# A seven-product down-projection whose partial sums are carried on by copies in PSUM

## The chip, the cores and the metric

The kernel runs on one core of a Trainium2 chip. The metric is the time of one execution on the device, in microseconds (us); less is better. Each run is one execution; a separate execution is recorded by the hardware profiler, and all rows quoted here are of that one.

## The reference

Tokens x of shape (2, 1, 4096, 640) go through two branches that a gate mixes per token. Branch A is a spectral block: a Fourier transform over the 4096 positions, a small two-layer complex network with soft thresholding per frequency and block of channels, and the inverse transform. Branch B is a gated feed-forward network with 640 channels and 1728 hidden units.

```python
def _A_ref(x, w1, b1, w2, b2):
    Xf = rfft2(x, axes=(1, 2))
    ...
    return irfft2(Yf, s=(H, W), axes=(1, 2))

def _B_ref(x, w_gate, w_up, w_down):
    return (_gelu(x @ w_gate) * (x @ w_up)) @ w_down

g = _sigmoid((x * gate_w).sum(-1, keepdims=True))
return g * _A_ref(...) + (1 - g) * _B_ref(...)
```

All of it is fp32.

## The kernel before

Every fp32 matrix product is made of three products of rounded parts (high x high, low x high, high x low). For an operand, ScalarE writes the high part (`high`, line 285) and VectorE subtracts it from the operand for the low part (`low`, line 288).

The change lies in the last stage, the down-projection together with the last step of the inverse transform. It runs in 32 iterations i, one for each batch b and each pair of token groups (na, 32 - na); an iteration makes two output rows, u1 and u2, of 128 tokens and 640 channels each. Iteration 0 has a branch of its own. The down-projection of an iteration is a 2 x 2 block product (two token groups, two halves of the hidden units, two halves c1, c2 of the channels) done with seven products in place of eight, after Winograd. The operands are the blocks a11, a12, a21, a22 of the hidden activations and sums of them: s3 = a11 - a21, s2 = a22 - s3, s1 = a11 + s2, s4 = a12 - s2. The weights are b11, b21, b22 and the combinations t1 to t4, made earlier. The seven products are a11 b11, s2 t2, s3 t3, a12 b21, s1 t1, a22 t4 and s4 b22, each of 20 or 21 matmuls of 128 x 320 into one PSUM bank. The sums that are wanted, with g1, g2 the gate of a token:

- u1, c1: a11 b11 + a12 b21
- u2, c2: a11 b11 + s2 t2 + s3 t3 + s1 t1
- u2, c1: a11 b11 + s2 t2 + s3 t3 + a22 t4
- u1, c2: a11 b11 + s2 t2 + s1 t1 + s4 b22

In an iteration the inverse transform (`inv2`, 12 matmuls of line 307, 24 where na is 0) comes first and leaves branch A's share in the SBUF tiles uu. Then `down` does six of the products in three pairs, with the matmuls of a pair interleaved over two banks (`duo`, line 1421), and the seventh alone (`run`, line 572). The partial sums that several outputs share go to an SBUF tile e: ScalarE copies a11 b11 there (line 1433), and VectorE adds s2 t2, s3 t3, a22 t4 and s4 b22 from their banks (lines 1437, 1442, 1478, 1490). VectorE also adds each finished sum, times the gate, to uu (`scaled`, line 1426), from a bank or from e.

The operands of later products are prepared between the products by `hooks[0]` to `hooks[7]`, which the program calls in the code's order:

- `h_op` makes the high and the low part of one block, tiles called ho in the profile. The low part is two or three VectorE instructions: a piece of 128 x 640 first, which the second matmul of a product already reads, and small ones.
- `h_s4` (VectorE, line 1350) makes s4; `h_s3`, `h_s2`, `h_s1` (GpSimd, lines 1332, 1339, 1344) make the sums for the next iteration n, two instructions each.
- `h_load`, `c_load` (SyncE's DMA queue) load the next iteration's blocks and its transformed rows; `v_load` (GpSimd's DMA queue, line 1194) loads the next matrix of the inverse transform; `c_split` makes four pairs of high and low parts of the transformed rows, called s2s.
- `st` notes a store of an output row, and `flush` (hooks 0 and 5) issues the noted ones on SyncE's queue.

Each engine works its queue in the order of the code and waits only for what an instruction needs: its operands, or the last reader of a buffer that it overwrites. GpSimd's queue in an iteration is: the DMA issue of v, h_s3, h_s2, h_s1.

Of the kernel before, what the change touches and what calls it, by code (L numbers as in the profile page):

```python
# [12 lines left out]
AF = mybir.ActivationFunctionType  # L13
# [208 lines left out]
def spectral_mix_kernel(ctx: ExitStack, tc: tile.TileContext, a):  # L222
    nc = tc.nc
    out = a["out"]
# [10 lines left out]
    def bank():  # L235
        return psum.tile([P, 512], F32, name="bank", tag="bank")
# [13 lines left out]
    def small(shape, dt=F32, name="small"):  # L250
        return pool.tile(shape, dt, name=name, tag="small", bufs=18)
# [7 lines left out]
    def st(dst, src):  # L259
        late.append((dst, src))  # L260
# [34 lines left out]
    def by_two(m):  # L295
        return m.rearrange("p (k i) -> p i k", k=2)
# [273 lines left out]
    def run(dst, ops, first=True):  # L570
        for i, (l, r) in enumerate(ops):
            nc.tensor.matmul(dst, l, by_two(r), start=first and i == 0, stop=i == len(ops) - 1, skip_group_check=True)  # L572
            while inner and i == 1:
                inner.pop()()
# [104 lines left out]

    PB, E = {}, []  # L680

# [289 lines left out]
    SC, Z, ZL1, ZL2, H, Y, NY = {}, {}, {}, {}, {}, {}, {}  # L971
# [214 lines left out]
    c_seq = [(b, na) for b in range(2) for na in range(16)]  # L1186
# [166 lines left out]
    def h_op(i, name, eng=nc.vector):  # L1353
        t = big([P, 5, 2, P], F32R, name="ho")
        uh, ul = (tiny([P, 2, P], F32R, name="ho") for k in range(2))
        src, six = HR[i].pop(name) if name in ("s1", "s3", "s4", "a22") else HR[i][name]
        split(t[:, :, 0], t[:, :, 1], src, eng)
        high(uh, six)
        if name in HALF:
            low(ul[:, 0], six[:, 0], uh[:, 0], eng)  # L1360
            low(uh[64:, 1], six[:64, 1], uh[:64, 1], eng)
        else:
            low(ul, six, uh, eng)
        HO[i, name] = [(t[:, j, 0], t[:, j, 1]) for j in range(5)] + [(uh[:, j], ul[:, j]) for j in range(2)]
# [25 lines left out]
                                               op0=OP.mult, op1=OP.add)  # L1390
        return uu

    def down(i, u, hooks):
        b, na = c_seq[i]
        n1, n2 = toks(na)
        g1, g2 = gs[:, b, 1, n1:n1 + 1], gs[:, b, 1, n2:n2 + 1]
        u1, u2 = u[n1], u[n2]
        c1, c2 = slice(0, 320), slice(320, 640)
        acc = lambda: bank()[:, :320]

        def rows(a_, b_):
# [10 lines left out]
        def duo(X, x, Y, y, hook, more=False):  # L1412

            n = [0, 0]
            hx, hy = rows(*x), rows(*y)
            tot = [sum(map(len, h)) for h in (hx, hy)]
            for j, (p, q) in enumerate(zip(hx, hy)):
                if j == 4:
                    hook()
                for k, (l, r) in ((0, p[0]), (0, p[1]), (1, q[0]), (0, p[2]), (1, q[-1]), *([(1, q[1])] if len(q) == 3 else ())):  # L1420
                    nc.tensor.matmul((X, Y)[k], l, by_two(r), start=n[k] == 0 and not (more and k), stop=n[k] == tot[k] - 1,  # L1421
                                     skip_group_check=True)
                    n[k] += 1

        def scaled(dst, x, g):
            nc.vector.scalar_tensor_tensor(dst, x, g, dst, op0=OP.mult, op1=OP.add)  # L1426
        hooks[0]()
        e = small([P, 2, 320], name="e")
        A = acc()
        if i:  # L1430
            Dd = acc()
            duo(A, ("a11", "b11"), Dd, ("a22", "t4"), hooks[1])
            nc.scalar.activation(e[:, 0], A, AF.Copy)
            hooks[2]()
            B, E = acc(), acc()
            duo(B, ("s2", "t2"), E, ("s1", "t1"), hooks[3])
            nc.vector.tensor_add(e[:, 0], B, e[:, 0])
            scaled(u2[:, c2], E, g2)
            hooks[4]()
            C = acc()  # L1440
            duo(C, ("s3", "t3"), A, ("a12", "b21"), hooks[5], True)
            nc.vector.tensor_add(e[:, 1], C, e[:, 0])
            scaled(u2[:, c2], e[:, 1], g2)
            scaled(u1[:, c1], A, g1)
        else:
            run(A, blk("a11", "b11"))
            nc.scalar.activation(e[:, 0], A, AF.Copy)
            hooks[1]()
            B = acc()
            run(B, blk("s2", "t2"))  # L1450
            nc.vector.tensor_add(e[:, 0], B, e[:, 0])
            hooks[2]()
            C = acc()
            run(C, blk("s3", "t3"))
            nc.vector.tensor_add(e[:, 1], C, e[:, 0])
            for u_, c_, x, g in ((u2, c2, 1, g2), (u2, c1, 1, g2), (u1, c2, 0, g1)):
                scaled(u_[:, c_], e[:, x], g)
            hooks[3]()
            F = acc()
            run(F, blk("s4", "b22"))  # L1460
            scaled(u1[:, c2], F, g1)
            hooks[4]()
            run(A, blk("a12", "b21"), first=False)
            scaled(u1[:, c1], A, g1)
            hooks[5]()
            Dd = acc()
            run(Dd, blk("a22", "t4"))
            scaled(u2[:, c1], Dd, g2)
            hooks[6]()
            E = acc()  # L1470
            run(E, blk("s1", "t1"))
            scaled(u1[:, c2], E, g1)
            st(out[b, n1], u1)
            scaled(u2[:, c2], E, g2)
            st(out[b, n2], u2)
            hooks[7]()
            return
        nc.vector.tensor_add(e[:, 1], Dd, e[:, 1])
        scaled(u2[:, c1], e[:, 1], g2)
        st(out[b, n2], u2)  # L1480
        hooks[6]()
        if i == len(c_seq) - 1:
            st(out[b, n1, :, c1], u1[:, c1])
            scaled(u1[:, c2], e[:, 0], g1)
            run(E, blk("s4", "b22"), first=False)
            scaled(u1[:, c2], E, g1)
            st(out[b, n1, :, c2], u1[:, c2])
            return
        run(E, blk("s4", "b22"), first=False)
        nc.vector.tensor_add(e[:, 0], E, e[:, 0])  # L1490
        scaled(u1[:, c2], e[:, 0], g1)
        st(out[b, n1], u1)
        hooks[7]()


# [79 lines left out]
    for k, (b, n2) in enumerate(a_seq):  # L1575
        i, j = steps_a[k]
# [46 lines left out]
    for i, key in enumerate(keys):  # L1623
# [18 lines left out]
        for j, t in enumerate(quads):  # L1642
            def hook(k):
                for f in slots.get((i, 7 * j + k), ()):
                    f()
# [7 lines left out]
            n = len(late)  # L1653
# [21 lines left out]
    uu, ahead = {}, {}  # L1675
    todo = {}
    for ch in range(1, 2 * NCH):
        b, c = chunks[ch]
# [23 lines left out]
    for i in range(S + 2):  # L1702
        events(i, 0)
        flush()
        if i < S:
# [5 lines left out]
            more = mlp1(*steps[i], sums if i + 1 < S else lambda: None)  # L1711
# [17 lines left out]


    SEQ = dict(enumerate(("s3", "s4", "a12", "a22", "s1")))
    DUO = {0: "s1", 2: "s3", 3: "a12", 4: "s4"}
    for i in range(len(c_seq)):
        n = i + 1 if i + 1 < len(c_seq) else None
        if i:
            uu = ahead if i == 1 else inv2(i)

        def step(k):
            def f():
                if (i, k) == (0, 0):  # L1740
                    wd_load(5, 5)
                    wd_later()
                if (i, k) == (0, 2):
                    ahead.update(inv2(1))
                if k in (0, 5):
                    flush()
                if k == (1 if i else 0):
                    h_s4(i)
                op = (SEQ if i == 0 else DUO).get(k)
# [22 lines left out]
        down(i, uu, [step(k) for k in range(8)])  # L1772
    flush()


# [19 lines left out]
```

## Time and profile before

| what | value |
|---|---|
| median of 3 runs | 2466.82 us (2465.4 to 2467.61) |
| the profiled execution | 2466.74 us, of which the span of the trace is 2465.0 us |
| down-projection, start of iteration 2 to start of iteration 31 | 1812.9 to 2439.3 us of the span |
| granted TensorE clock | 1.0 throughout |

A row of the timeline reads: start, length in us, engine, line, operation, what it writes and reads (buffer numbers left out), shape, count of equal instructions merged in the row, and in brackets how long the engine had been idle and what ended that. In a row of a group the numbers behind the bar are its busy time, the mean length of one in ns, and the idle time ahead of it. PE is TensorE, PEld its weight loads, DVE VectorE, ACT ScalarE, POOL GpSimd, SP SyncE.

### The profile page before, as it was taken

The page shows a single profiled execution, that of the slowest core. Times are in us where ns is not written, and L with a number is a line of the kernel's source. Part 1 is how long each engine was busy: PE and PEld are TensorE (multiplying, and loading weights), DVE is VectorE, ACT ScalarE, POOL GpSimd, SP SyncE. Part 2 cuts the span into 40 slices and gives each one's busy share as a digit, 9 for nine tenths or more (in the row PEclk, how much of TensorE's full clock was granted, in tenths as well). Part 3 has the DMA queues.
Part 4 walks back from the last instruction along what each step waited for, and adds up shares of the span by engine and source line. Part 5 has one row for each costly group of instructions (what it writes and reads, how often), then busy time and mean ns, then how long its engine had stood idle before and what let it go on. Part 6 is the DMA issues. An engine that isn't in the chain of part 4 may idle for free.

```text
span 2465.0 us, 54653 instructions
## 1 busy us (share of the span) xinstructions
PE 2445.0 (99%) x20239; PEld 2430.0 (99%) x20239; DVE 2065.8 (84%) x4323; ACT 1486.9 (60%) x3503; POOL 390.5 (16%) x404
## 2 busy tenths in 40 slices
PE   9999999999999999999999999999999999999999
PEld 9999999999999999999999999999999999999999
DVE  7777788777777877877767888888899999999998
ACT  5555556666666666666556788888744454455443
POOL 0111100000000000000003111111043334333342
PEclk9999999999999999999999999999999999999999
DMA  6666667777778687777677446467854444544443
GB/s 208 212 229 214 242 208 232 224 263 236 250 236 261 196 257 250 237 227 248 222 234 234 148 139 174 147 173 244 308 176 145 140 150 156 167 161 153 148 145 112
DMA packets 351422, 499.50 MB, mean 203 GB/s; under 512 B 26028, under 2 KB 223276, under 8 KB 351156
## 3 DMA queue, kind: packets, MB, share of 16 engines
q1 hardware_dynamic: 333684, 445.02, 56.1%
q0 software_dynamic: 17472, 51.00, 5.7%
q8 instruction: 159, 2.61, 0.4%
q14 instruction: 107, 0.88, 0.1%
HBM read 307.10 MB, written 188.81 MB: 201 GB/s over the span
## 4 chain that ended last, share of the span: by engine, by line
PE 71%; DVE 19%; issue 5%; DMA 3%; ACT 2%; SPq 0%; DVEq 0%; ACTq 0%
PE bank L572 48%; PE bank L307 11%; DVE ho L288 7%; PE bank L1421 6%; DVE s2s L288 3%; PE bank L993 3%; DVE uu L1426 2%; PE bank L704 2%; DVE uu L1389 1%; PE bank L827 1%; DVE hs L1350 1%; DMA s<-scr 1%; PE bank L1079 0%; PE bank L1080 0%; DMA xraw<-in_xT_dram 0%
## 5 line engine op out<-in xcount | busy, mean ns | idle before, releaser
L572 PE MATMUL bank<-xo,w 128*128 128x256 f32 x11196 | 1298.3, 275 | 3.1 <-ACT u L598 1.5
L572 PEld LDWEIGHTS bank<-xo,w 128*128 128x128 f32 x11196 | 1276.1, 192 | 5.9 <-ACT u L598 2.1
L1421 PE MATMUL bank<-wx,ho 128*128 128x320 f32 x3844 | 532.4, 300 | 5.6 <-DVE ho L288 5.5
L1421 PEld LDWEIGHTS bank<-wx,ho 128*128 128x128 f32 x3844 | 524.4, 189 | 10.2 <-DVE ho L288 10.0
L285 ACT ACTIVATE ho<-hraw 128x640 fp32r<-128x640 f32 x320 | 168.3, 574 | 118.5 <-PE bank L1421 83.7
L288 DVE TENSOR_TENSOR ho<-hraw,ho 128x640 fp32r<-128x640 f32 (+3 forms) x384 | 226.8, 632 | 6.4 <-ACT ho L285 3.4
L598 ACT ACTIVATE u<-bank 128x256 f32<-128x256 f32 x328 | 125.4, 382 | 161.2 <-PE bank L572 154.7
L288 DVE TENSOR_TENSOR xs<-xr,xs 64x640 fp32r<-64x640 f32 x128 | 105.0, 820 | 75.9 <-ACT xs L285 73.4
L650 DVE TENSOR_TENSOR u<-bank,u 128x256 f32<-128x256 f32 x204 | 85.9, 421 | 79.8 <-ACT u L598 78.7
L288 DVE TENSOR_TENSOR xo<-xraw,xo 128x512 fp32r<-128x512 f32 x194 | 133.3, 688 | 17.0 <-ACT xo L285 15.7
L307 PE MATMUL bank<-wm,h 128*128 128x320 f32 (+1 forms) x792 | 129.7, 300 | 0.5 <-DVE h L1057 0.4
L829 DVE TENSOR_TENSOR as<-bank,as 64x320 f32<-64x320 f32 x256 | 113.9, 484 | 18.3 <-ACT as L828 16.4
L285 ACT ACTIVATE xo<-xraw 128x512 fp32r<-128x512 f32 x194 | 121.7, 627 | 8.4 <-DMA xraw<-in_xT_dram 7.3
L598 ACT ACTIVATE p<-bank 128x256 f32<-128x256 f32 x144 | 55.3, 384 | 104.6 <-DVE h L661 57.7
L288 DVE TENSOR_TENSOR s2s<-s,s2s 128x320 fp32r<-128x320 f32 x128 | 115.7, 963 | 2.4 <-ACT s2s L285 1.5
L307 PEld LDWEIGHTS bank<-wm,h 128*128 128x128 f32 (+1 forms) x792 | 111.8, 186 | 2.1 <-DVE h L1057 0.6
L572 PE MATMUL bank<-wx,ho 128*128 128x320 f32 x764 | 110.4, 300 | 0.9 <-DVE ho L288 0.9
L285 ACT ACTIVATE xs<-xr 64x640 fp32r<-64x640 f32 x128 | 93.9, 734 | 28.2 <-DMA xr<-in_x_dram 26.4
L828 ACT ACTIVATE as<-bank 64x320 f32<-64x320 f32 x256 | 96.9, 427 | 20.3 <-PE bank L827 15.4
L572 PEld LDWEIGHTS bank<-wx,ho 128*128 128x128 f32 x764 | 105.7, 189 | 2.1 <-DVE ho L288 2.1
L780 POOL MEMSET h<- 64x512 f32 x16 | 8.3, 522 | 614.2 <-DVE h L665 178.2
L599 ACT ACTIVATE h<-bank 128x256 f32<-128x256 f32 x204 | 77.8, 381 | 29.4 <-PE bank L572 27.8
(196 smaller groups left out, 3892.8 us busy)
## 6 DMA issues: line engine op xcount, KB each, us to landing
xo<-xD SPq DMA_DIRECT2D x124, 512.0 KB
xraw<-in_xT_dram SPq DMA_DIRECT2D x215, 256.0 KB
hD<-h SPq DMA_DIRECT2D x184, 256.0 KB
hraw<-hD SPq DMA_DIRECT2D x128, 320.0 KB
xD<-xo POOLq DMA_DIRECT2D x64, 512.0 KB, 3.6
sc<-scr SPq DMA_DIRECT2D x65, 320.0 KB
xr<-in_x_dram SPq DMA_DIRECT2D x64, 320.0 KB
scr<-as SPq DMA_DIRECT2D x64, 320.0 KB
```

The source lines that it names most:

```text
L285: nc.scalar.activation(dst, src, AF.Copy, scale=scale)
L288: eng.tensor_sub(dst, src, hi.bitcast(F32))
L307: nc.tensor.matmul(dst, l, by_two(r), start=i == 0, stop=i == len(ops) - 1)
L572: nc.tensor.matmul(dst, l, by_two(r), start=first and i == 0, stop=i == len(ops) - 1, skip_group_check=True)
L598: copy = lambda d, s_: nc.scalar.activation(d, s_, AF.Copy)
L599: gelu = lambda d, s_: nc.scalar.activation(d, s_, AF.Gelu_apprx_tanh)
L650: nc.vector.tensor_add(u4, C, u4)
L704: nc.tensor.matmul(acc, l, by_two(r), start=first and i == 0, stop=i == 2, skip_group_check=True)
L828: nc.scalar.activation(stg[hi, cs], pa[lo, :320], AF.Copy)
L829: nc.vector.tensor_add(stg[hi, cs], pa[hi, :320], stg[hi, cs])
L993: nc.tensor.matmul(pz.rearrange("p (r e k f) -> p k r e f", r=2, e=2, k=4)[:, kp], SC[b, c, kp][:, o:o + P], ft.rearrange("p (r e f) -> p ...
L1421: nc.tensor.matmul((X, Y)[k], l, by_two(r), start=n[k] == 0 and not (more and k), stop=n[k] == tot[k] - 1, skip_group_check=True)
```

## The change

For iterations 1 to 31 the seven products are done one by one, in the order a11 b11, s2 t2, a12 b21, s3 t3, s1 t1, a22 t4, s4 b22, and the tile e is gone. Three PSUM banks, taken in iteration 0 and written there by matmuls, stay reserved as B, C and E2. ScalarE copies the bank of a11 b11 (A) to B; s2 t2 is added onto B by TensorE; ScalarE copies B to C; s3 t3 is added onto C; ScalarE copies C to E2; a22 t4 is added onto E2, s4 b22 onto B, a12 b21 onto A. VectorE then only adds finished banks, times the gate, to uu: six instructions in place of nine. s1 t1 has a bank of its own, E, which is added to two outputs. The inverse transform of the iteration is called behind a11 b11 and the first copy (`between`). The operands are prepared in the order of their new use, and h_s4 and s4's parts follow accordingly.

```diff
+            B, C, E2 = seeds
+            A = acc()
+            run(A, blk("a11", "b11"))
+            nc.scalar.activation(B, A, AF.Copy)
+            u = between()
...
+            hooks[1]()
+            run(B, blk("s2", "t2"), first=False)
+            nc.scalar.activation(C, B, AF.Copy)
+            hooks[2]()
+            run(A, blk("a12", "b21"), first=False)
+            scaled(u1[:, c1], A, g1)
+            hooks[3]()
+            run(C, blk("s3", "t3"), first=False)
+            nc.scalar.activation(E2, C, AF.Copy)
...
+            scaled(u2[:, c2], C, g2)
+            hooks[4]()
+            E = acc()
+            run(E, blk("s1", "t1"))
+            scaled(u2[:, c2], E, g2)
+            scaled(u1[:, c2], E, g1)
+            hooks[5]()
+            run(E2, blk("a22", "t4"), first=False)
+            scaled(u2[:, c1], E2, g2)
+            st(out[b, n2], u2)
+            hooks[6]()
+            run(B, blk("s4", "b22"), first=False)
+            scaled(u1[:, c2], B, g1)
...
-            duo(A, ("a11", "b11"), Dd, ("a22", "t4"), hooks[1])
-            nc.scalar.activation(e[:, 0], A, AF.Copy)
...
-            duo(B, ("s2", "t2"), E, ("s1", "t1"), hooks[3])
-            nc.vector.tensor_add(e[:, 0], B, e[:, 0])
...
-            duo(C, ("s3", "t3"), A, ("a12", "b21"), hooks[5], True)
-            nc.vector.tensor_add(e[:, 1], C, e[:, 0])
...
-    DUO = {0: "s1", 2: "s3", 3: "a12", 4: "s4"}
+    LATER = {0: "a12", 1: "s3", 2: "s1", 3: "a22", 4: "s4"}
...
-                if k == (1 if i else 0):
+                if k == (3 if i else 0):
                     h_s4(i)
...
                     if k == 6:
-                        h_op(n, "a22")
+                        h_op(n, "s2")
                         h_s1(n, nc.gpsimd)
-                    if k == 7:
-                        h_op(n, "s2")
```

What stands in the queues then, first on VectorE, ahead of the low part of s4 (the last operand of an iteration). In the names, ho<-hraw and ho<-hs are low parts of blocks, s2s<-s those of the transformed rows, hs<-hraw is h_s4, and uu<-bank a scaled sum. Before, from the low part of s3 on:

```order
L288 TENSOR_TENSOR ho<-hraw,ho 128x5x128
L288 TENSOR_TENSOR ho<-hraw,ho 128x256
L288 TENSOR_TENSOR ho<-hraw,ho 128x5x128
L288 TENSOR_TENSOR ho<-hraw,ho 128x128
L288 TENSOR_TENSOR ho<-hraw,ho 64x128
L288 TENSOR_TENSOR s2s<-s_30887,s2s 128x320
L288 TENSOR_TENSOR s2s<-s_30889,s2s 128x320
L288 TENSOR_TENSOR s2s<-s_30887,s2s 128x320
L288 TENSOR_TENSOR s2s<-s_30889,s2s 128x320
L1437 TENSOR_TENSOR e<-bank,e 128x320
L1426 SCALAR_TENSOR_TENSOR uu<-bank,gs,uu 128x320
L288 TENSOR_TENSOR ho<-hs,ho 128x5x128
```

The first two are s3, the next three a12; the addition into e waits for the product s2 t2. On VectorE after, from the scaled sum of A on:

```order
L1416 SCALAR_TENSOR_TENSOR uu<-bank,gs,uu 128x320
L1350 TENSOR_TENSOR hs<-hraw,hs 128x640
L1350 TENSOR_TENSOR hs<-hraw,hs 128x256
L288 TENSOR_TENSOR ho<-hraw,ho 128x5x128
L288 TENSOR_TENSOR ho<-hraw,ho 128x128
L288 TENSOR_TENSOR ho<-hraw,ho 64x128
L288 TENSOR_TENSOR s2s<-s_30506,s2s 128x320
L288 TENSOR_TENSOR s2s<-s_30508,s2s 128x320
L288 TENSOR_TENSOR s2s<-s_30506,s2s 128x320
L288 TENSOR_TENSOR s2s<-s_30508,s2s 128x320
L1416 SCALAR_TENSOR_TENSOR uu<-bank,gs,uu 128x320
L288 TENSOR_TENSOR ho<-hs,ho 128x5x128
```

The first row waits for the end of a12 b21; h_s4 now stands behind it, then the low part of a22, the four s2s and the scaled sum of C (which waits for s3 t3), and then s4's low part. On GpSimd, one iteration before, with the engines or queues waited for:

```order
L1194 DMA v<-in_v_dram 128x256 [waits DVE_49]
L1332 TENSOR_TENSOR hraw<-hraw 128x640 [waits DMAHW7_49,DMAHW1_49]
L1332 TENSOR_TENSOR hraw<-hraw 128x256 [waits DMAHW2_49,DMAHW0_49]
L1339 TENSOR_TENSOR hs<-hraw 128x640 [waits DMAHW3_49,Pool_49]
L1339 TENSOR_TENSOR hs<-hraw 128x256 [waits DMAHW4_49,PE_49,Pool_49]
L1344 TENSOR_TENSOR hraw<-hs,hraw 128x640 [waits DVE_49,Pool_49]
L1344 TENSOR_TENSOR hraw<-hs,hraw 128x256 [waits DMASW2_49,DVE_49,Pool_49]
```

On GpSimd after, the same seven:

```order
L1194 DMA v<-in_v_dram 128x256 [waits PE_49]
L1332 TENSOR_TENSOR hraw<-hraw 128x640 [waits DMAHW7_49,DMAHW3_49,DMAHW1_49]
L1332 TENSOR_TENSOR hraw<-hraw 128x256 [waits DMAHW2_49,DMAHW0_49,DMASW5_49]
L1339 TENSOR_TENSOR hs<-hraw 128x640 [waits DMAHW3_49,DVE_49,Pool_49]
L1339 TENSOR_TENSOR hs<-hraw 128x256 [waits DVE_49,DMAHW4_49,Activation_49,Pool_49]
L1344 TENSOR_TENSOR hraw<-hs,hraw 128x640 [waits DVE_49,Pool_49]
L1344 TENSOR_TENSOR hraw<-hs,hraw 128x256 [waits DVE_49,Pool_49]
```

Their order stays. The buffer that v is loaded into was last read by VectorE's low part of s3 before; after, it is a small tile of a12 that TensorE reads last, in the seventeenth of the 20 matmuls of a12 b21.

More of the change, by code (lines that the diff above doesn't have):

```diff
@@ L1428, in down @@
+        u1, u2 = u[n1], u[n2]
         e = small([P, 2, 320], name="e")
         A = acc()
-        if i:
-            Dd = acc()
-            duo(A, ("a11", "b11"), Dd, ("a22", "t4"), hooks[1])
-            nc.scalar.activation(e[:, 0], A, AF.Copy)
-            hooks[2]()
-            B, E = acc(), acc()
-            duo(B, ("s2", "t2"), E, ("s1", "t1"), hooks[3])
-            nc.vector.tensor_add(e[:, 0], B, e[:, 0])
-            scaled(u2[:, c2], E, g2)
-            hooks[4]()
-            C = acc()
-            duo(C, ("s3", "t3"), A, ("a12", "b21"), hooks[5], True)
-            nc.vector.tensor_add(e[:, 1], C, e[:, 0])
[L1443 to L1477, printed above, removed]
@@ L1491, in down @@
-        scaled(u1[:, c2], e[:, 0], g1)
-        st(out[b, n1], u1)
+        run(A, blk("a11", "b11"))
+        nc.scalar.activation(e[:, 0], A, AF.Copy)
+        hooks[1]()
+        B = seeds[0]
+        run(B, blk("s2", "t2"))
+        nc.vector.tensor_add(e[:, 0], B, e[:, 0])
+        hooks[2]()
+        C = seeds[1]
+        run(C, blk("s3", "t3"))
+        nc.vector.tensor_add(e[:, 1], C, e[:, 0])
+        for u_, c_, x, g in ((u2, c2, 1, g2), (u2, c1, 1, g2), (u1, c2, 0, g1)):
+            scaled(u_[:, c_], e[:, x], g)
@@ new lines, in down @@
+        hooks[3]()
+        F = acc()
+        run(F, blk("s4", "b22"))
+        scaled(u1[:, c2], F, g1)
+        hooks[4]()
+        run(A, blk("a12", "b21"), first=False)
+        scaled(u1[:, c1], A, g1)
+        hooks[5]()
+        Dd = seeds[2]
+        run(Dd, blk("a22", "t4"))
+        scaled(u2[:, c1], Dd, g2)
+        hooks[6]()
+        E = acc()
+        run(E, blk("s1", "t1"))
+        scaled(u1[:, c2], E, g1)
+        st(out[b, n1], u1)
+        scaled(u2[:, c2], E, g2)
+        st(out[b, n2], u2)
```

45 lines of the change are left out of this document (16 added, 29 removed).

## The prediction

> **What bounds the kernel now.** I read the page first, then the last stage by itself.
>
> ```profile
> span 2465.0 us, 54653 instructions
> PE 2445.0 (99%) x20239; PEld 2430.0 (99%) x20239; DVE 2065.8 (84%) x4323; ACT 1486.9 (60%) x3503; POOL 390.5 (16%) x404
> ```
>
> The share of TensorE says little about who sets the pace, so the next view is the table of stretches, cut from the start of iteration 2 of the down-projection to the start of iteration 31 (columns: length, then busy time of PE, PEld, DVE, ACT and POOL, the granted clock, DMA).
>
> ```profile
> 1812.90:2439.30 626.40, 621.80 (x4539) 616.84 (x4538) 614.01 (x1041) 308.78 (x667) 238.39 (x203) 1.00 0.46 154
> ```
>
> VectorE is busy 614.0 of 626.4 us (98%), ScalarE 49%, GpSimd 38%. Two engines are full here, TensorE and VectorE. TensorE's timeline tells which waits for which.
>
> ```profile
> 1793.91 16.43 PE L1421 MATMUL bank<-wx,ho 128*128 128x320 f32 x119 [0.82 <-DVE ho L288]
> ...
> 1812.89 1.79 PE L307 MATMUL bank<-s2s,v 128*128 128x320 f32 x12
> ...
> 1857.34 0.84 PE L1421 MATMUL bank<-wx,ho 128*128 128x320 f32 x5
> 1858.68 16.43 PE L1421 MATMUL bank<-wx,ho 128*128 128x320 f32 x119 [0.50 <-DVE ho L288]
> ...
> 1899.86 1.79 PE L307 MATMUL bank<-s2s,v 128*128 128x320 f32 x12
> 1901.49 17.04 PE L1421 MATMUL bank<-wx,ho 128*128 128x320 f32 x124
> 1918.37 2.88 PE L572 MATMUL bank<-wx,ho 128*128 128x320 f32 x20
> 1921.08 1.79 PE L307 MATMUL bank<-s2s,v 128*128 128x320 f32 x12
> ...
> 2115.30 3.42 PE L307 MATMUL bank<-s2s,v 128*128 128x320 f32 x24
> ...
> 2439.28 1.79 PE L307 MATMUL bank<-s2s,v 128*128 128x320 f32 x12
> ...
> 2441.94 16.43 PE L1421 MATMUL bank<-wx,ho 128*128 128x320 f32 x119 [0.19 <-DVE ho L288]
> ```
>
> An iteration without a wait lasts 1921.08 - 1899.86 = 21.22 us for 156 matmuls, 0.136 each. The 29 iterations from 1812.89 to 2439.28 take 626.39 us; 29 x 21.22 and 1.63 for the 12 extra matmuls of the row with x24 make 617.0. The rest, 9.4 us, is waiting, always at the sixth matmul of the first pair of products, for the low part of a22 from VectorE. With 0.8 in iteration 1 and 0.2 in iteration 31 that is 10.4 us: all that this stage can give back if its matmuls stay the same. Without it the execution would take 2466.7 - 10.4 = 2456.3 us.
>
> **The change, part by part.** The sum is made against the profiled execution, 2466.74 us, 0.1 below the median of the runs.
>
> Matmuls: the same seven products and the same 12 for the inverse transform, 156 per iteration. That products come one after another costs nothing: the 20 matmuls of s4 b22 already run alone on one bank, 1918.37 to 1921.08, 0.136 each, as in the pairs.
>
> VectorE's combining work, priced by shape in that stretch (busy us, mean ns):
>
> ```profile
> L288 DVE TENSOR_TENSOR ho<-hraw,ho 128x640 fp32r<-128x640 f32 x145 | 118.9, 820 | 4.4 <-ACT ho L285 3.4
> L1426 DVE SCALAR_TENSOR_TENSOR uu<-e,gs,uu 128x320 f32<-128x320 f32 x88 | 71.7, 814 | 3.1
> L1426 DVE SCALAR_TENSOR_TENSOR uu<-bank,gs,uu 128x320 f32<-128x320 f32 x58 | 31.2, 538 | 0.0
> L1490 DVE TENSOR_TENSOR e<-bank,e 128x320 f32<-128x320 f32 x29 | 14.3, 492 | 0.9
> L1478 DVE TENSOR_TENSOR e<-bank,e 128x320 f32<-128x320 f32 x29 | 13.8, 475 | 0.0
> L1433 ACT ACTIVATE e<-bank 128x320 f32<-128x320 f32 x29 | 12.7, 437 | 123.6 <-PE bank L1421 123.6
> ```
>
> Before: four additions of 0.48, three scaled sums from e of 0.81, two from a bank of 0.54, 5.4 us. After: six from a bank, 3.2 us. VectorE gets 2.2 us per iteration back. ScalarE gets two copies more of some 0.44, 0.9 us on an engine that is half idle. Copying onto a bank has no row; bounds are 0.44 and, taken as slow as the slowest other bank read of that size here, 0.54. I take 0.44; either is covered, since between a copy's source and the product that adds onto it lie 12, 20 and 21 matmuls (1.6 to 2.9 us). Only iteration 1, whose inverse transform was done early, has nothing between: 0.7 us once (copy and two hand-overs).
>
> So far this reads as a gain. What speaks against it is when VectorE's work falls, and what GpSimd does then. Two stretches of the timeline:
>
> ```profile
> 2127.73 1.70 DVE L288 TENSOR_TENSOR s2s<-s,s2s 128x320 fp32r<-128x320 f32 x4
> ...
> 2129.93 2.24 POOL L1332 TENSOR_TENSOR hraw<-hraw 128x640 f32<-128x640 f32 x2
> 2130.17 0.54 DVE L1426 SCALAR_TENSOR_TENSOR uu<-bank,gs,uu 128x320 f32<-128x320 f32 x1
> 2130.62 4.93 DVE L288 TENSOR_TENSOR ho<-hs,ho 128x640 fp32r<-128x640 f32 x3
> 2132.12 2.23 POOL L1339 TENSOR_TENSOR hs<-hraw 128x640 f32<-128x640 f32 x2
> ...
> 2168.93 2.41 DVE L288 TENSOR_TENSOR ho<-hraw,ho 128x640 fp32r<-128x640 f32 x5
> ...
> 2172.23 2.79 POOL L1332 TENSOR_TENSOR hraw<-hraw 128x640 f32<-128x640 f32 x2 [1.27 <-DMA hraw<-hD]
> ...
> 2175.21 3.05 DVE L288 TENSOR_TENSOR ho<-hs,ho 128x640 fp32r<-128x640 f32 x3
> ...
> 2182.57 1.34 DVE L288 TENSOR_TENSOR ho<-hraw,ho 128x640 fp32r<-128x640 f32 x3
> ...
> 2188.91 1.15 DVE L1350 TENSOR_TENSOR hs<-hraw,hs 128x640 f32<-128x640 f32 x2
> ...
> 2189.98 3.80 DVE L288 TENSOR_TENSOR ho<-hraw,ho 128x640 fp32r<-128x640 f32 x5
> 2191.43 0.57 POOL L1194 DMA_DIRECT2D v<-in_v_dram  x1 [9.64 <-DVE ho L288]
> 2192.09 2.28 POOL L1332 TENSOR_TENSOR hraw<-hraw 128x640 f32<-128x640 f32 x2
> 2193.81 4.01 DVE L288 TENSOR_TENSOR s2s<-s,s2s 128x320 fp32r<-128x320 f32 x4
> ...
> 2198.60 1.33 DVE L288 TENSOR_TENSOR ho<-hs,ho 128x640 fp32r<-128x640 f32 x3
> ```
>
> The same four s2s subtractions take 1.70 us alone and 4.01 beside GpSimd; the same three pieces of s4's low part 1.33 and 4.93. The scaled sum at 2130.17, which reads a bank, takes its usual 0.54 under a running GpSimd instruction. So a VectorE instruction with two SBUF tensors stands still while GpSimd computes, and one with a PSUM operand does not. From 2189.98 to the end of s4's low part at 2199.93 VectorE takes 9.95 us. Free, the same row of work is 2.41 + 1.70 + 0.48 + 0.54 + 1.33, less 0.08 for each of four overlaps, 6.14. Price of GpSimd's four subtractions (h_s3, h_s2): 3.8 us. From 2168.93, where GpSimd came late (DMA), to 2178.26 it is 9.33, a price of 3.2.
>
> The Trainium skill (SBUF — State Buffer, section "SBUF: two separate sides") calls the port pair of the two engines an exclusive lock, held for a whole instruction, which blocks the loser fully. That rule would charge the four at full length, 2.24 + 2.23 = 4.5 us, and the sum below would end at 2509 by it; the rows charge 3.8.
>
> Now the new order on VectorE. The scaled sum of A waits for the end of a12 b21; behind it, in order, stand h_s4 (1.15), a22's low part (1.34), the four s2s (1.70), the scaled sum of C (0.54), and the first piece of s4's low part (0.82), which TensorE needs at the second matmul of the seventh product. Free: 0.54 + 1.15 + 1.34 + 1.70 + 0.54 + 0.82 less five overlaps of 0.08 is 5.7, and 0.1 to wake, 5.8 us. TensorE, from the end of a12 b21, has s3 t3, s1 t1, a22 t4 and one matmul to do, 63 x 0.136 = 8.6 us. That would fit. But GpSimd's release moves too: its queue has v's DMA issue first, which waited for the low part of s3 and now waits for the seventeenth matmul of a12 b21, 0.4 us ahead of that product's end. With 0.3 to wake (as now: s3's two pieces end 1.15 after 2189.98, v follows at 2191.43) and 0.57 for the issue, h_s3 starts 0.6 us after the end of a12 b21, unless its operands land later.
>
> When they land hangs on SyncE, which issues the loads behind the two stores of the iteration before. A row of it (both stores), and two of ScalarE, whose high parts come ahead of VectorE's low parts:
>
> ```profile
> 2161.63 2.70 SPq L264 DMA_DIRECT2D out_dram<-uu  x2
> ...
> 2188.97 1.97 ACT L285 ACTIVATE ho<-hraw 128x640 fp32r<-128x640 f32 x4
> 2190.84 1.54 ACT L285 ACTIVATE s2s<-s 128x320 fp32r<-128x320 f32 x4
> ```
>
> Now the second store is out at 2164.3 and the latest h_s3 starts 7.9 us behind it, at 2172.23, held by its operands. In the new order the second store needs the sum of B. From the first piece of s4's low part VectorE has 0.5 of that part, two sums of E (1.1), a11's pair (1.15), the sum of E2 (0.5), s2's pair (1.15) beside h_s1 (some 1.6) and the sum of B (0.5) ahead of it: 6.5, less some 0.5 of overlaps, while TensorE needs 2.6 for the rest of s4 b22: the store goes 3.4 us into the next iteration. With 7.9 that is 11.3; a12 b21 ends 74 x 0.136 = 10.1 into it. So h_s3 starts 0.6 to 1.2 us after that product's end, and all four subtractions fall into it: 5.8 + 3.8 and some 0.05 to restart TensorE make 9.65, and TensorE stands 9.65 - 8.57 = 1.08 us before s4 b22, in each iteration.
>
> Bounds of that wait: 0.5 with the late GpSimd's 3.2, 1.75 with 4.5, nothing if GpSimd came so late that s4's part is ready first. I take 3.8, since GpSimd starts as early in the row as at 2192.09. The rest of the period has room: a11's low part, the tightest, is out half a microsecond ahead of its product, and VectorE is idle about 1 us before it waits for A again. ScalarE's 1.97 and 1.54 (high parts and s2s) fill 3.5 of the 5.6 us between two of its copies, so it is not late.
>
> Sum: 2456.3 (all present waits gone) + 30 iterations with a follower x 1.08 = 32.4 + 0.7 = 2489 us, 0.9% slower.
>
> **Rivals.** *VectorE's relief decides.* If no more than 2.7 us of GpSimd's work falls ahead of s4's low part, TensorE never waits and the time is 2456 to 2458, 0.4% faster. For it: 2.2 us of VectorE's 21 per iteration go, and every present wait is for VectorE. Against it: the place of v's issue, which puts h_s3 right at the head of the row. It decides above 2.7 us. The Trainium skill (Perfetto Trace Analysis, Optimizing Scalar/DVE Operations) has the same rule: where VectorE is saturated, move work to ScalarE. By it this rival would be the forecast.
>
> *The lock is longer.* A piece blocked by all four, as at 2130.62, stops h_s4 and with it a22's low part too; a wait of 1.75 per iteration, 2456.3 + 52.5 + 0.7 = 2509.
>
> *The copies are late.* If ScalarE reached each of three copies only when TensorE wants it, 0.44 + 0.3 three times in 31 iterations, 69 us, 2525. Against it: 3.5 us of its own work between copies 5.6 us apart. Here belongs the skill's advice to rotate products through banks so that a copy hides (Perfetto Trace Analysis, Optimizing Tensor Performance); the chain keeps other products between.
>
> **How the numbers follow.** A wait of 0.5 to 1.75 before s4 b22: 0.75, of which 0.1 near the long end (0.5 gives 2456.3 + 15 + 0.7 = 2472); late copies 0.03; relief 0.15; between relief and the forecast, a wait near 0.35, which just repays the gain: 0.07. A measurement of this kernel tells 0.2% (4.9 us) from nothing. The range leaves out the copies, the far end of the lock and a little of the relief: 2458 to 2509; the likeliest case alone is 2472 to 2509.
>
> **What would show it.** Right: PE waits `<-DVE ho` of about 1 us ahead of one product in each iteration, the wait at the sixth matmul gone, VectorE at 93 to 96%, GpSimd's h_s3 beginning within 2 us of the scaled sum of A, s2s and h_s4 slow beside it. Wrong: h_s3 seen 4 us or more behind that sum, or the s2s back at 0.43 each.

## The result: 2499.6 us, 1.3% slower

The changed kernel takes 2499.57 us (median of 4 runs, 2498.80 to 2500.68), the kernel before, beside it, 2467.05: ratio 1.0133, 95% interval [1.0116, 1.0151]. The forecast was 2489, the range 2458 to 2509.

Page of the changed kernel's profiled execution (2500.68 us), span and engines:

```profile
span 2498.9 us, 54472 instructions
PE 2452.7 (98%) x20239; PEld 2431.1 (97%) x20239; DVE 2056.6 (82%) x4230; ACT 1504.0 (60%) x3565; POOL 395.0 (16%) x404
```

VectorE has 9.2 us less to do in all and the kernel is slower. The table of stretches, cut as before from one inverse transform to another, that of iteration 2 to that of iteration 31 (length, then PE, PEld, DVE, ACT, POOL):

```profile
1812.34:2476.57 664.23, 630.56 (x4539) 619.04 (x4538) 610.17 (x955) 327.12 (x725) 243.09 (x203) 1.00 0.43 145
```

664.2 us where there were 626.4; VectorE is at 92% where it was at 98%. With 617.0 us of matmuls in the 29 iterations, TensorE now stands 47.2 us, 1.63 per iteration; before it was 9.4. Its timeline shows where:

```profile
2157.36 1.79 PE L307 MATMUL bank<-s2s,v 128*128 128x320 f32 x12
2158.99 11.57 PE L572 MATMUL bank<-wx,ho 128*128 128x320 f32 x84
2170.77 2.98 PE L572 MATMUL bank<-wx,ho 128*128 128x320 f32 x20 [0.21 <-DVE ho L288]
2174.76 5.70 PE L572 MATMUL bank<-wx,ho 128*128 128x320 f32 x40 [1.00 <-DVE ho L288]
2180.30 1.79 PE L307 MATMUL bank<-s2s,v 128*128 128x320 f32 x12
2181.93 14.62 PE L572 MATMUL bank<-wx,ho 128*128 128x320 f32 x104
2197.54 5.70 PE L572 MATMUL bank<-wx,ho 128*128 128x320 f32 x40 [0.99 <-DVE ho L288]
2203.07 1.79 PE L307 MATMUL bank<-s2s,v 128*128 128x320 f32 x12
...
2476.57 1.79 PE L307 MATMUL bank<-s2s,v 128*128 128x320 f32 x12
```

The stop ahead of the row with x40 is the second matmul of s4 b22 (19 of that product, then 21 of the next a11 b11); the one ahead of the row with x20 is a22 t4. The brackets give less than the loss: 20 matmuls take 2.72 us, and from 2170.77 to 2174.76 there are 3.99, a loss of 1.27 where the row shows 1.00. The list of waits has the same two views for the whole stretch, and PEld, the weight loads, comes nearer to 47.2:

```profile
PEld bank L572 <- DVE ho L288: 45.2, 48, 2.2
PE bank L572 <- DVE ho L288: 33.6, 46, 1.9
```

VectorE and GpSimd in the first of these iterations, from the scaled sum of A on:

```profile
2164.63 0.57 POOL L1194 DMA_DIRECT2D v<-in_v_dram  x1 [9.24 <-PE bank L572]
2164.76 0.55 DVE L1416 SCALAR_TENSOR_TENSOR uu<-bank,gs,uu 128x320 f32<-128x320 f32 x1 [0.47 <-PE bank L572]
2165.22 2.23 POOL L1332 TENSOR_TENSOR hraw<-hraw 128x640 f32<-128x640 f32 x2
2165.23 4.75 DVE L1350 TENSOR_TENSOR hs<-hraw,hs 128x640 f32<-128x640 f32 x2
2167.41 1.55 POOL L1339 TENSOR_TENSOR hs<-hraw 128x640 f32<-128x640 f32 x1
2169.91 1.33 DVE L288 TENSOR_TENSOR ho<-hraw,ho 128x640 fp32r<-128x640 f32 x3
2171.27 2.24 DVE L288 TENSOR_TENSOR s2s<-s,s2s 128x320 fp32r<-128x320 f32 x4
2171.47 0.88 POOL L1339 TENSOR_TENSOR hs<-hraw 128x256 f32<-128x256 f32 x1 [2.51 <-ACT ho L285]
2173.43 0.54 DVE L1416 SCALAR_TENSOR_TENSOR uu<-bank,gs,uu 128x320 f32<-128x320 f32 x1
2173.89 1.33 DVE L288 TENSOR_TENSOR ho<-hs,ho 128x640 fp32r<-128x640 f32 x3
```

GpSimd issues v and starts h_s3 0.46 us after the scaled sum of A. VectorE's h_s4, 1.15 us when free, takes 4.75: its first piece waits until three GpSimd instructions are through; the four s2s take 2.24 instead of 1.70, beside the fourth. The first piece of s4's low part is out at 2174.70 (2173.89 and 0.81), 9.94 us after 2164.76, and TensorE goes on at 2174.76.

Not every iteration is like this one. Of the 28 between 1835 and 2470 us, 16 have the long hold (h_s4's first piece 4.4 us, row 9.92 to 9.94). In ten, h_s3 starts 0.5 to 3.0 us behind the scaled sum, when that piece has already started, and the piece takes its free 0.82; nine of these have a row of 9.34 to 9.58. The mean row is 9.79.

### The profile page after: what moved, and what is told of

The parts are those of the page before. It is cut to its first block, busy times and chain, and to the rows that moved or that the text cites. A ratio compares the mean times of both kernels' runs of the same rounds, so it can differ in the third digit from the quotient of the medians.

```text
span 2498.9 us, 54472 instructions
## 1 busy us (share of the span) xinstructions
PE 2452.7 (98%) x20239; PEld 2431.1 (97%) x20239; DVE 2056.6 (82%) x4230; ACT 1504.0 (60%) x3565; POOL 395.0 (16%) x404
## 4 chain that ended last, share of the span: by engine, by line
PE 80%; DVE 14%; DMA 2%; ACT 2%; issue 2%; SPq 0%; DVEq 0%; POOL 0%; ACTq 0%
PE bank L572 60%; PE bank L307 12%; DVE hs L1350 4%; DVE ho L288 3%; DVE s2s L288 3%; PE bank L993 3%; PE bank L704 2%; PE bank L827 1%; DMA hraw<-hD 1%; DVE uu L1416 1%; PE bank L1079 1%; PE bank L1080 1%; DMA xraw<-in_xT_dram 0%; DMA scr<-as 0%; DVE w L288 0%
## 5 line engine op out<-in xcount | busy, mean ns | idle before, releaser
L288 DVE TENSOR_TENSOR ho<-hraw,ho 128x640 fp32r<-128x640 f32 (+3 forms) x384 | 216.9, 599 | 37.0 <-ACT ho L285 35.0
L285 ACT ACTIVATE ho<-hraw 128x640 fp32r<-128x640 f32 x320 | 163.1, 572 | 9.6 <-DMA hraw<-hD 4.0
L1422 ACT ACTIVATE bank<-bank 128x320 f32<-128x320 f32 x31 | 13.1, 422 | 201.8 <-DVE uu L1416 193.4
L288 DVE TENSOR_TENSOR ho<-hs,ho 128x640 fp32r<-128x640 f32 (+3 forms) x160 | 125.7, 816 | 4.0 <-ACT ho L285 2.9
L1416 DVE SCALAR_TENSOR_TENSOR uu<-bank,gs,uu 128x320 f32<-128x320 f32 x191 | 101.4, 545 | 20.1 <-PE bank L572 18.6
L1350 DVE TENSOR_TENSOR hs<-hraw,hs 128x640 f32<-128x640 f32 x64 | 111.4, 1780 | 0.0
L1344 POOL TENSOR_TENSOR hraw<-hs,hraw 128x640 f32<-128x640 f32 (+1 forms) x62 | 88.8, 1450 | 139.7 <-DVE ho L288 139.7
```

What stands on the lines that cost most here:

```text
L285: nc.scalar.activation(dst, src, AF.Copy, scale=scale)
L288: eng.tensor_sub(dst, src, hi.bitcast(F32))
L1344: eng.tensor_add(d["a11"][k], d["s2"][k], d["a11"][k])
L1350: nc.vector.tensor_sub(d["s2"][k], d["a12"][k], d["s2"][k])
```

## The experiments

Theory 1: the row on VectorE from the scaled sum of A to s4's low part, made longer by GpSimd's subtractions, sets the iteration. Rival 2: ScalarE's copies and the hand-overs round them cost the time. Rival 3: products one at a time on one bank are slower for TensorE. Since the stages ahead, which no run changes, end anywhere from 1759.9 to 1764.2 us, the last column has the last stage alone: span less the start of its first row with 24 matmuls of the inverse transform (before: 2465.0 - 1764.24; after: 2498.9 - 1761.53). Less its waits of 10.4, the stage of the kernel before is 690.4: the floor (an estimate; the run without h_s3 ends 1.0 below it, with iterations of 21.19 us where 21.22 were counted).

| run | time, us | ratio to before, 95% interval | last stage, us |
|---|---|---|---|
| before | 2464.6 to 2467.1 (medians beside the runs) | 1 | 700.8 |
| changed kernel | 2499.57 | 1.0133 [1.0116, 1.0151] | 737.4 |
| h_s4 early | 2466.90 | 1.0008 [0.9999, 1.0017] | 704.3 |
| s2s split late | 2471.26 | 1.0027 [1.0016, 1.0038] | 707.7 |
| no h_s3 (work left out) | 2451.76 | 0.9947 [0.9933, 0.9960] | 689.4 |
| copies, old order | 2460.65 | 0.9985 [0.9977, 0.9994] | 696.3 |
| new order, no copies | 2508.28 | 1.0179 [1.0164, 1.0193] | 743.4 |
| v behind h_s3, h_s2 | 2487.82 | 1.0093 [1.0078, 1.0107] | 724.5 |
| h_s4 early, half of the split late | 2454.83 | 0.9961 [0.9947, 0.9975] | 690.9 |
| split late, two banks B | 2470.25 | 1.0018 [1.0009, 1.0027] | 706.4 |
| h_s4 early, half of the split late, no copies | 2482.26 | 1.0067 [1.0051, 1.0084] | 717.8 |

### h_s4 out of the row

```diff
-                if k == (3 if i else 0):
+                if k == (2 if i else 0):
                     h_s4(i)
```

> The changed kernel with h_s4 (VectorE, 1.15 us free) one step earlier, at the head of step 2 in place of step 3: out of the row between the scaled sum of A and s4's low part, into the 1.2 us per iteration that VectorE stands there before the low part of s1 (33.2 us over 28 iterations, waiting for ScalarE's high part). Theory 1 (the row on VectorE, with GpSimd's four subtractions in it, sets the iteration): the waits before a22 t4 and s4 b22 (22.9 or 22.6 us per iteration where 21.2 are matmuls) shrink by about 1.1 in each of 30 iterations: 2499.6 - 33 = 2466 us (2460 to 2472); GpSimd then holds up a22's low part and s2s instead. Rival 2 (ScalarE's copies and the hand-overs around them cost the time): ScalarE's order is untouched, 2495 to 2502. Rival 3 (products one at a time on one bank are slower for TensorE): 2495 to 2502.

Measured: 2466.90, as theory 1 has it; the copies and the products are the same, so rivals 2 and 3 fall. TensorE's timeline, and VectorE's groups (busy, mean ns) from 1835 to 2425 us:

```profile
1850.12 5.70 PE L572 MATMUL bank<-wx,ho 128*128 128x320 f32 x40 [0.38 <-DVE ho L288]
1871.96 5.70 PE L572 MATMUL bank<-wx,ho 128*128 128x320 f32 x40 [0.38 <-DVE ho L288]
```

```profile
L288 DVE TENSOR_TENSOR ho<-hraw,ho 128x640 fp32r<-128x640 f32 x137 | 176.1, 1285 | 3.6 <-ACT ho L285 3.6
L1350 DVE TENSOR_TENSOR hs<-hraw,hs 128x640 f32<-128x640 f32 x27 | 22.1, 818 | 0.0
```

Most iterations are 21.84 us, 0.62 above their matmuls. h_s4's large piece is back at 0.82; GpSimd now holds a22's low part, in the group of 128x640 pieces (1.29 on average; the kernel before had 0.82).

### h_s3 left out

```diff
-                        h_s3(n, nc.gpsimd)
+                        if i:
+                            HR[n]["s3"] = HR[n].pop("a21")
+                        else:
+                            h_s3(n, nc.gpsimd)
                         h_s2(n, nc.gpsimd)
```

> The changed kernel with h_s3 (GpSimd's first two subtractions, 2.2 us of its 4.5 in the row) left out from the third token pair on, so s3 is the plain a21 block there; the output is not the reference's. VectorE's, ScalarE's and TensorE's instructions are all the same. Theory 1 (VectorE stands still while GpSimd computes): the row gets about 2.2 us shorter, more than the loss of 1.35 to 1.7, and h_s4's large piece falls from 2.9 to 4.4 us to about 2: 2456 to 2461 us. Rival 1 (the row is too long by VectorE's own work, GpSimd runs beside it for nothing): 2495 to 2501. Rivals 2 and 3: 2495 to 2501.

Measured: 2451.76, the stage at 689.4. Iterations 2 to 30 have no wait left (first from 1812.66 on, behind the transform):

```profile
1812.66:2427.19 614.53, 614.53 (x4527) 614.53 (x4525) 548.85 (x951) 322.27 (x722) 179.52 (x145) 1.00 0.46 156
```

Nothing but two GpSimd instructions per iteration is gone (and with them the right output). That VectorE's own work made the row too long is excluded, and with it rivals 2 and 3 for the waits: with all copies and all single products, TensorE runs without a stop, 21.19 us per iteration.

### v's issue behind the subtractions

```diff
                         if k == 3:
-                            v_load(n)
+                            if i == 0:
+                                v_load(n)
                             c_split(n)
                     if k == 4:
                         h_s3(n, nc.gpsimd)
                         h_s2(n, nc.gpsimd)
+                        if i and n > 1:
+                            v_load(n)
```

> The changed kernel with one row of GpSimd's queue moved: v's DMA issue behind h_s3 and h_s2, no longer ahead of them. All other queues are the same. Theory 1, with the prediction's step that v's issue (it waits for the seventeenth matmul of a12 b21) puts h_s3 at the head of the row: h_s3 starts when its operands land, up to 1.2 us earlier, so part of GpSimd's 4.5 us falls into the 1.2 and 0.5 us that VectorE stands ahead of the scaled sum of A: 0.3 to 1.2 less wait in each of 30 iterations, 2464 to 2491 us. If the loads behind the two stores release h_s3 (the prediction's other gate), nothing: 2495 to 2502. If v then comes late for the inverse transform, slower than 2502.

Measured: 2487.82, 11.8 us less than the changed kernel, 0.4 per iteration. GpSimd and VectorE in one iteration:

```profile
1866.27 2.82 POOL L1332 TENSOR_TENSOR hraw<-hraw 128x640 f32<-128x640 f32 x2 [7.92 <-DMA hraw<-hD]
1866.50 2.86 DVE L1350 TENSOR_TENSOR hs<-hraw,hs 128x640 f32<-128x640 f32 x2
1869.05 3.01 POOL L1339 TENSOR_TENSOR hs<-hraw 128x640 f32<-128x640 f32 x2
1869.29 3.23 DVE L288 TENSOR_TENSOR ho<-hraw,ho 128x640 fp32r<-128x640 f32 x3
```

The loads now release h_s3, 0.23 us behind the scaled sum of A, which started at 1866.04. Both gates of the prediction exist. In this row v's was the later one by about 0.2 us, and in 18 of the 28 iterations of the changed kernel h_s3 starts at once behind v's issue; in the other ten it comes later. The row gets shorter by some 0.5 (in most iterations 9.2 to 9.5 from the scaled sum of A to the end of s4's first piece, 9.33 on average where the changed kernel has 9.79). Not all of that is the earlier start: here h_s4's first piece is never held for more than 2.2 us, as by one GpSimd instruction, where the changed kernel has 4.4.

### The s2s split out of the row, and why it doesn't reach the floor

```diff
                             v_load(n)
-                            c_split(n)
+                        if k == (6 if i else 3):
+                            c_split(n)
```

> The changed kernel with c_split (four s2s high parts on ScalarE, four low parts on VectorE, 1.70 us free) moved from step 3 to step 6, behind s4's and a11's low parts and ahead of s2's. Theory 1 (row on VectorE): 1.7 us leave the row, more than the 1.35 to 1.7 that TensorE loses per iteration, so the wait ahead of s4 b22 goes; what is left is VectorE's total, 21.2 busy of 22.9 us, against TensorE's 21.2: 2456 to 2468 us, 2461 likeliest. If GpSimd's lock finds the moved work too, or s2s come late for the inverse transform, up to 2480. Rivals 2 and 3 (copies, single products): 2495 to 2502.

Measured: 2471.26, above the 2456 to 2468 of theory 1. The wait at s4 b22 goes, as expected, and another comes, which no theory had named. Rows of one iteration, VectorE, ScalarE and TensorE:

```profile
1836.03 0.54 DVE L1416 SCALAR_TENSOR_TENSOR uu<-bank,gs,uu 128x320 f32<-128x320 f32 x1
...
1836.66 0.42 ACT L1422 ACTIVATE bank<-bank 128x320 f32<-128x320 f32 x1 [5.77 <-DVE uu L1416]
...
1837.14 1.08 PE L572 MATMUL bank<-wx,ho 128*128 128x320 f32 x6 [0.29 <-ACT bank L1422]
```

The copy of A onto B's bank starts 0.09 us after VectorE has taken the scaled sum of the old B, which stands behind the moved s2s on its queue; TensorE waits for the copy. The 0.09 us are the same in every iteration from the second on. A second bank for B, used by turns, was to free it:

```diff
-            seeds.extend(acc() for k in range(3))
+            seeds.extend(acc() for k in range(4))
...
-            B, C, E2 = seeds
+            B, C, E2 = seeds[3 * (i % 2)], seeds[1], seeds[2]
```

> The run with the late split (2471.3 us; TensorE stood 0.3 to 0.4 us before the second product, for ScalarE's copy of A onto B) with two banks for B by turns. Theory 4 (that copy is late since B is held until VectorE has taken the scaled sum of B of the iteration before): the copy goes free, 2451 to 2458 us. Rival (ScalarE itself is late with that copy, behind its high parts): 2467 to 2473. With one bank fewer to turn, the inverse transform's second pair could wait for VectorE: 2475 or above.

Measured: 2470.25, no gain, and a time that the rival had named. But the rival is wrong: the copy now starts at 1835.88, behind its own product and 3.26 us after VectorE's last scaled sum, and nothing waits for it, as theory 4 said. With one bank fewer in turn, the second pair of the inverse transform waits for ScalarE to empty one (the third case had named VectorE, and 2475 or above), and that costs as much:

```profile
1835.68 1.39 PE L307 MATMUL bank<-s2s,v 128*128 128x320 f32 x9
1837.29 0.68 PE L307 MATMUL bank<-s2s,v 128*128 128x320 f32 x3 [0.22 <-ACT uu L1388]
1837.80 19.72 PE L572 MATMUL bank<-wx,ho 128*128 128x320 f32 x144
1857.36 1.39 PE L307 MATMUL bank<-s2s,v 128*128 128x320 f32 x9
```

### Half of the split late, h_s4 early: faster than both kernels

```diff
-                if k == (3 if i else 0):
+                if k == (2 if i else 0):
                     h_s4(i)
...
                             v_load(n)
-                            c_split(n)
+                            c_split(n, slice(0, 2 if i else 4))
+                        if k == 6 and i:
+                            c_split(n, slice(2, 4))
```

> The run with h_s4 early (2466.9 us, 0.37 shown and some 0.6 lost ahead of s4 b22 per iteration) with, besides, two of the four s2s splits moved from step 3 to step 6: 0.85 us more out of the row, and half of what the run with the late split put on VectorE's tail. Theory 1: the wait ahead of s4 b22 goes (0.85 > 0.6), the copy onto B is not yet late (in the run with all four late it lost 0.3 to 0.4 in each iteration): 2450 to 2456 us, 0.4% to 0.5% below the kernel before and below all runs so far with the full work. If the tail is as full with half of it: 2458 to 2465.

Measured: 2454.83, 0.39% below the kernel before. The stage takes 690.9, the floor within 0.5; TensorE's rows follow each other without a bracket from iteration 2 on:

```profile
1834.25 1.79 PE L307 MATMUL bank<-s2s,v 128*128 128x320 f32 x12
1835.88 19.72 PE L572 MATMUL bank<-wx,ho 128*128 128x320 f32 x144
1855.44 1.79 PE L307 MATMUL bank<-s2s,v 128*128 128x320 f32 x12
```

### Copies without the order, the order without copies

The copies alone, in the old order with its pairs (cut; `lead` blocks of the second product come first, `on` says which bank is added onto):

```diff
+            B, E = acc(), acc()
+            nc.scalar.activation(B, A, AF.Copy)
-            duo(B, ("s2", "t2"), E, ("s1", "t1"), hooks[3])
-            nc.vector.tensor_add(e[:, 0], B, e[:, 0])
+            duo(B, ("s2", "t2"), E, ("s1", "t1"), hooks[3], (1, 0), 3)
+            C = acc()
+            nc.scalar.activation(C, B, AF.Copy)
+            scaled(u1[:, c2], B, g1)
...
-            duo(C, ("s3", "t3"), A, ("a12", "b21"), hooks[5], True)
-            nc.vector.tensor_add(e[:, 1], C, e[:, 0])
-            scaled(u2[:, c2], e[:, 1], g2)
+            duo(C, ("s3", "t3"), A, ("a12", "b21"), hooks[5], (1, 1), 3)
+            scaled(u2[:, c2], C, g2)
```

> The kernel before, its order of work and its pairs kept, with the copies alone: A copied to B's bank, B to C's by ScalarE, the products added on by TensorE; the second product of a pair starts three blocks (nine matmuls) ahead, which covers the copy, and the low parts of s3 and a12 change places for that. VectorE has seven scaled sums from banks, 3.8 us, in place of 5.4. Theory 1 (the copies help, the new order costs): VectorE, 21.2 us busy per iteration before, falls to 19.6, the wait at a22's low part goes: 2456 to 2460 us, 0.3 to 0.4% below the kernel before. Rival 2 (copies and their hand-overs cost): 0.7 us or more exposed at each of two copies in 30 iterations, 2500 or above. Rival 3 tells nothing here, the products are in pairs.

Measured: 2460.65, 0.15% below the kernel before; 0.7 us outside what was expected, since the low part of s4 is now late by a little in 19 of 29 iterations (waits from 1812 to 2435 us):

```profile
PEld bank L572 <- DVE ho L288: 6.2, 19, 0.4
```

So in the old order the copies help, by 4.5 us of stage, together with the earlier start of the second products and the exchange of two low parts that come with them; no run has these without the copies. The new order with the products one by one, but with VectorE's additions as before (cut):

```diff
-            nc.scalar.activation(B, A, AF.Copy)
+            nc.scalar.activation(e[:, 0], A, AF.Copy)
...
-            run(C, blk("s3", "t3"), first=False)
-            nc.scalar.activation(E2, C, AF.Copy)
+            run(C, blk("s3", "t3"))
+            nc.vector.tensor_add(e[:, 1], C, e[:, 0])
...
-            scaled(u2[:, c2], C, g2)
+            scaled(u2[:, c2], e[:, 1], g2)
```

> The new order and the products one by one, without the chained copies: every product starts its bank fresh, VectorE adds the partial sums in an SBUF tile as in the kernel before (four additions of 0.48, three scaled sums from e of 0.81 in place of three of 0.54: 2.7 us more VectorE per iteration than in the changed kernel), ScalarE has two copies fewer. Theory 1 (VectorE's row sets the iteration): the row gets 0.75 longer (one addition of C, one scaled sum from e), and VectorE's total goes from 21.2 to 23.9 per iteration against 22.8 that the changed kernel takes: 2522 to 2560 us, about 2540; so the copies pay in this order, and the order costs more than the changed kernel's 33 us. Rival 2 (the copies and their hand-overs cost the time): faster than the changed kernel, about 2460 to 2480. Rival 3 (single products): about 2500, nothing but the products matters.

Measured: 2508.28: slower than the changed kernel, so rival 2 falls once more, but by 9 us (6 of stage) where 22 to 60 were expected. Rows of one iteration show why:

```profile
1843.00 0.55 DVE L1416 SCALAR_TENSOR_TENSOR uu<-bank,gs,uu 128x320 f32<-128x320 f32 x1 [0.27 <-PE bank L572]
1843.47 2.51 DVE L1350 TENSOR_TENSOR hs<-hraw,hs 128x640 f32<-128x640 f32 x2
1844.09 2.49 POOL L1332 TENSOR_TENSOR hraw<-hraw 128x640 f32<-128x640 f32 x2 [0.66 <-DMA hraw<-hD]
...
1851.84 0.55 DVE L1416 SCALAR_TENSOR_TENSOR uu<-e,gs,uu 128x320 f32<-128x320 f32 x1
...
1855.56 2.53 POOL L1344 TENSOR_TENSOR hraw<-hs,hraw 128x640 f32<-128x640 f32 x2 [5.31 <-DVE ho L288]
...
1856.18 1.32 DVE L1416 SCALAR_TENSOR_TENSOR uu<-e,gs,uu 128x320 f32<-128x320 f32 x1
```

A scaled sum from e takes 0.55, the same as one from a bank, and 1.32 beside GpSimd; the 0.81 of the sum of before was a mean of the two. And GpSimd starts 1.09 us behind the scaled sum of A, held by its loads, so h_s4's first piece escapes. The row has 10.1 us here, and on average 0.2 more than the changed kernel's. Against the kernel before, which makes the same additions, the new order with single products costs 42.6 us of stage (743.4 against 700.8); the copies win back 6.0 of it.

What the copies are worth where the row no longer binds, told by taking them out of the best run (the edit of the run before, made on top of the best one):

> The best run so far (h_s4 early, two s2s splits late, 2454.8 us) with the chained copies taken out again: fresh banks, partial sums added by VectorE in an SBUF tile. It tells what the copies are worth where the row no longer binds. Theory 1, by VectorE's total: 570.9 us of 590 in the best run, 20.5 per iteration; four additions of 0.48 and three scaled sums from e of 0.55 to 0.80 against six sums from a bank where there were three more of 0.54 add 2.0 to 2.7 us, less the overlaps, 0.1 to 0.2; 22.3 to 23.0 per iteration against TensorE's 21.2: 2454.8 + 30 x (1.1 to 1.8) = 2488 to 2509 us. If GpSimd's hold falls on fewer instructions in the longer row, as in the run with the order alone, 22.0 and 2475 to 2488. Rival (the copies are worth nothing, the row was all): 2453 to 2459.

Measured: 2482.26, 27 us more than with the copies; the second case, 2475 to 2488, came true, not the 2488 to 2509 of theory 1. From 1835 to 2425 us VectorE is full, 98%, and its scaled sums from e are held:

```profile
1835.00:2425.00 590.00, 577.80 (x4168) 567.26 (x4167) 580.26 (x982) 294.94 (x617) 222.38 (x187) 1.00 0.46 152
```

```profile
L1418 DVE SCALAR_TENSOR_TENSOR uu<-e,gs,uu 128x320 f32<-128x320 f32 x80 | 75.3, 942 | 2.8
```

## Why the prediction came out as it did

The sign, the place and the mechanism were right; the wait was put at 1.08 us per iteration and is 1.63.

- *The row ahead of s4 b22* (forecast 9.65 with its hand-overs): shown by moving each of its parts. Taking h_s4, the s2s or h_s3 out of it gave 33, 30 and 48 us of stage back.
- *The price of GpSimd in the row* was taken as 3.8 us. In 16 of 28 iterations the row is 9.93 us where its free length is 5.7: 4.2. In the nine of 9.34 to 9.58, where h_s4's first piece starts ahead of h_s3, it is 3.6 to 3.9, as forecast; on average (9.79) it is 4.1. That is the first mis-sized term, 0.3 of the 0.55. In the row of the kernel before, at 2189.98, a VectorE instruction got through behind each GpSimd instruction; in the 16, one VectorE instruction waited for three. Why it is one and not the other was not settled. The rival with the longer lock (1.75, 2509) described the place better, h_s4 held by several instructions in one go, at a price half-way between.
- *Hand-overs* were 0.15: 0.1 to wake VectorE and 0.05 for TensorE, both without a row behind them. From the end of a12 b21 (2158.99 + 41 x 0.136 = 2164.57) to the scaled sum are 0.19, then 0.06 to TensorE, and 0.1 more are lost in the rows after each stop (40 matmuls, 5.54 from 2174.76 to 2180.30 instead of 5.44). That is the other 0.2. Check: 0.19 + 9.94 + 0.06 - 8.57 + 0.1 = 1.72; the iteration from 2157.36 to 2180.30 is 22.94, 1.72 above 21.22.
- *When GpSimd starts*: forecast 0.6 to 1.2 us after the end of a12 b21, measured 0.65 (2165.22 - 2164.57) where v's issue is the gate, in 18 of 28 iterations, and more in the other ten. That v's issue is a gate was shown by moving it, though in this row the loads come only some 0.2 us ahead of it.
- *VectorE's relief of 2.2 us per iteration* was too large: three scaled sums from e at 0.81 were priced with GpSimd's hold in them. With 0.55 it is 1.4 (4 x 0.48 + 3 x 0.55 + 2 x 0.54 less 6 x 0.54). The sum did not rest on it, the rival of the relief did; that rival was refuted by the changed kernel. Where the row does not bind, the times come near its 2456 to 2458: 2460.65 with the copies in the old order, 2454.83 with the row repaired.
- *Copies hidden, products one by one free*: right. The copy onto a bank takes 0.42 us (0.44 assumed), and nothing waits for it in the changed kernel but iteration 1, 0.63 (0.7 forecast). What the prediction did not name is that a copy waits for the bank's last reader, VectorE; that bound the run with the split late. (In the changed kernel, too, the copy onto B starts 0.1 us behind that reader, but early enough for TensorE.)
- *Signs*: the wait at the sixth matmul is gone, but a22's low part still stops TensorE in over half of the iterations (0.2 shown); VectorE is at 92%, not 93 to 96, as the iteration is longer than forecast. In the kernel before, the wait was not always at a22's low part, as the prediction had it: the weight loads show 0.9 us, in four waits, ahead of the product done alone, s4 b22.

The sum counted 30 iterations with a stop; iteration 1 has none at s4 b22 (its 144 matmuls from 1792.33 on run through), so 29 pay. The sum was 690.4 + 33.1 for the stage and came to 737.4, 13.9 more; 2.7 of it are hidden in the time because the unchanged stages ended that much earlier in this execution (1761.53 against 1764.24).

The Trainium skill (SBUF — State Buffer, section "SBUF: two separate sides") has the lock exclusive and held for a whole instruction: by it the four subtractions cost 4.5. The trace has 4.2 in 16 iterations and 4.1 on average, between that and the 3.8 taken. The advice of the Trainium skill to move work to ScalarE where VectorE is saturated (Perfetto Trace Analysis, Optimizing Scalar/DVE Operations) agrees with the pair of runs in which nothing else moved, -27 us with the copies in the best run; in the old order, where a little else moved, it is -4.5 us of stage.

## What to carry to other kernels

Where two engines hold each other up, cost a reordering by what lies between a product's end and the next operand that TensorE needs, with the other engine's whole instructions in it, and look up what releases that engine; an engine's total busy time says nothing about such a row. Moving work off a full engine and moving its order are two changes: time each alone, since here the copies were worth 4 to 27 us and the order, with its single products, cost 43. A bank that is kept and copied into waits for its last reader, so whatever delays that reader delays the chain.

## What was not expected of the hardware

- One VectorE instruction was held through three GpSimd instructions in a row, which the prediction had as a rival only: h_s4's 128 x 640 piece, 0.82 us free, is the most of the 4.75 us of the pair at 2165.23. From 1835 to 2425 us it takes 4.4 us in 14 of 26 iterations and 0.82 in ten, so its mean of 2.88 is the length of none of these:

```profile
L1350 DVE TENSOR_TENSOR hs<-hraw,hs 128x640 f32<-128x640 f32 x26 | 75.0, 2884 | 0.0
```

- A mean duration can have the other engine's hold in it: the scaled sum from e is 0.55 alone, 1.32 beside GpSimd, 0.81 or 0.94 on average.
